# Half-row pairs for one term of two units, a split logarithm and a new step order in a convolution and feed-forward kernel

## Chip, cores and metric

The kernel runs on one core of a Trainium2 chip. The metric is the device time of one execution in microseconds (us). TensorE is called PE here (its weight loads PEld), VectorE DVE, ScalarE ACT, GpSimd POOL, and SyncE, which only issues DMAs in this kernel, SP.

## What is computed

An input of 8 x 4096 tokens with 192 features passes a causal convolution with 7 taps, whose weights are a softmax for each of 8 heads (24 features per head). Then comes a feed-forward layer with a rational function between its two products:

```python
w = np.exp(w - max(w)); w = w / (np.sum(w) + 1e-9)          # per head, over 7 taps
out = np.einsum('hk,bskhg->bshg', w, x_unf)                  # convolution, 192 features per token
x = out.reshape(32768, 192)
h = x @ w_in                                                 # 192 -> 2048
P = a[0] + a[1]*h + a[2]*h**2 + a[3]*h**3
Q = 1.0 + abs(b[0])*abs(h) + abs(b[1])*h**2
g = P / (Q + 1e-6)
y = g @ w_out                                                # 2048 -> 192
```

## The kernel before

The 32768 tokens are cut into 64 **chunks** of 512 tokens, and the 2048 columns of the hidden layer into 8 **units** of 256, as two halves j = 0, 1 of 128. A step is written as kind, number, piece and chunk. In a chunk the following happens.

The convolution (`conv_step`, step `c`, L312) multiplies banded weights with blocks of the input. It splits the array by `tile_position` into two row halves of 64 and four column groups of 32: 72 f32 matmuls of 58 (at the end 48) columns, each of them two instructions, in eight parts. ACT rounds its result to `xh0`, `xh1` (step `xh`, L330), DVE takes the remainder `xl` (step `xl`, L339), and 14 small DMAs (`gaps`, `move`, L352) put the features in order. `X[c, "A"]` holds the rounded features 0 to 127, `X[c, "L"]` their remainders. `X[c, "B"]` holds the rounded features 128 to 191 in rows 0 to 63 and their remainders in rows 64 to 127; the weights of these features stand in both row halves.

The first product (`gemm1`, steps `g1` + unit + piece: `g15b` is unit 5, half 1; L369) has **five terms** of 128x128 weights and 512 columns for each half: high weights with A, low weights with A, high weights with L, high weights with B, low weights with B. They are summed in one PSUM bank of `hp`; `ps_h` has two buffers, so unit k needs the buffer of unit k-2.

Each unit's `hp` goes through `hs` (ACT copy, L410), `p` and `u` (POOL, L413, L417), `A` and `B` (ACT, L424, L427), `v` (DVE, L421, the last reader of `hp`), `Q` (a DMA issued by POOL that adds B to A, L430), `L` (ACT, logarithm over 1024 columns, L433), `Y` (ACT, exponential, L436), `m`, `e`, `g` (DVE, L440, L444, L448). A step `g` + unit without a piece, as `g1.2`, is the DVE step; `g1` with a piece, as `g16a`, is the first product, and `g2` with a piece, as `g20a`, the second one (`gemm2`, L387), with f32 weights and 192 columns, 16 instructions per unit. `O` is the evacuation of the output (ACT, L397; DMA by SP, L398).

The order of all steps on PE, ACT, DVE and POOL is written out by hand, as text: `START` for the first chunks with the preparation of the weights (steps `w..`; L284 is one of them, and their scratch buffers are those of the convolution from chunk 1 on), `PLAN`, repeated for each chunk i from 3 to 62, and `END`. In PLAN the number behind the point says how many chunks the step is late: `c0.0` is the convolution of chunk i, `g15b.1` belongs to chunk i-1, `g16a.2` to chunk i-2. So PE runs `... g15a.1 g15b.1 | c0.0 g16a.2 g16b.2 ...` at the border of two rounds. Each engine executes its steps in the order of the text and waits only for what a step reads or overwrites. In END the number counts back from chunk 64.

Of the kernel before, what the change touches and what calls it, by code (L numbers as in the profile page):

```python
# [41 lines left out]


PLAN = """
c0.0 xh0.0 xh1.0 g16a.2 g16b.2 m2.2 L3.2 xl0.0 xl1.0 B5.2 A5.2 g20b.2 e2.2 g2.2 p5.2 u5.2 g20a.2 hs6.2
Y3.2 g20c.2 g21a.2 g21c.2 v5.2 Q5.2 p6.2 A6.2 u6.2 g20d.2 m3.2 g17a.2 g17b.2 e3.2 g22a.2 L4.2 g3.2 B6.2
hs7.2 v6.2 g21b.2 Y4.2 g21d.2 g22b.2 L5.2 m4.2 Q6.2 e4.2 B7.2 A7.2 g10a.1 g10b.1 g4.2 p7.2 g22d.2 g23b.2
g23d.2 g24b.2 hs0.1 u7.2 p0.1 Y5.2 A0.1 v7.2 L6.2 B0.1 m5.2 e5.2 Q7.2 g11a.1 g11b.1 hs1.1 g22c.2 g5.2
u0.1 g23a.2 g23c.2 g24a.2 Y6.2 p1.1 Q0.1 v0.1 g12a.1 g12b.1 g24d.2 B1.1 A1.1 L7.2 m6.2 e6.2 g6.2 hs2.1
g25b.2 u1.1 Q1.1 p2.1 Y7.2 v1.1 B2.1 m7.2 u2.1 e7.2 g24c.2 g25a.2 A2.1 g13a.1 g13b.1 L0.1 g7.2 hs3.1  # L50
Q2.1 Y0.1 p3.1 g25c.2 g26a.2 v2.1 g26c.2 g27a.2 m0.1 L1.1 A3.1 g14a.1 g14b.1 B3.1 u3.1 Q3.1 e0.1 g27c.2
# [9 lines left out]
wor0.0 wiw4.0 g10b.0 wio3.0 wod1.0 hs0.0 B0.0 wow2.0 woa1.0 p0.0 u0.0 wip1.0 A0.0 Q0.0 wir3.0 wid4.0
wil1.0 wos1.0 woo1.0 wia4.0 g11a.0 g11b.0 hs1.0 p1.0 tp7.0 B1.0 wor1.0 wip2.0 wis4.0 wio4.0 woa2.0
wil2.0 u1.0 A1.0 Q1.0 wos2.0 woo2.0 v0.0 wih3.0 wip3.0 wiw5.0 wia5.0 wod2.0 L0.0 wow3.0 wis5.0 wor2.0
wil3.0 wiw6.0 wid5.0 Y0.0 wio5.0 woa3.0 wow4.0 g12a.0 wir4.0 g12b.0 v1.0 hs2.0 p2.0 wos3.0 m0.0 B2.0
g13a.0 g13b.0 woo3.0 u2.0 wih4.0 wip4.0 wia6.0 wod3.0 L1.0 wor3.0 wiw7.0 A2.0 e0.0 wis6.0 g0.0 hs3.0
# [5 lines left out]
xh0.2 xh1.2 m3.0 xl0.2 e3.0 g3.0 g20a.0 g20c.0 B6.0 hs7.0 p6.0 u6.0 v6.0 g21a.0 g21c.0 g22a.0 L4.0
g10a.1 g10b.1 xl1.2 g20b.0 Q6.0 p7.0 g20d.0 Y4.0 g21b.0 u7.0 m4.0 B7.0 g21d.0 g22b.0 wor4.0 A7.0 Q7.0
L5.0 L6.0 e4.0 hs0.1 g4.0 Y5.0 wod5.0 v7.0 g11a.1 p0.1 m5.0 e5.0 u0.1 wod6.0 B0.1 A0.1 g11b.1 Q0.1 hs1.1
p1.1 A1.1 g5.0 Y6.0 v0.1 m6.0 e6.0 g22c.0 g23a.0 L7.0 u1.1 g22d.0 g23b.0 wor6.0 g6.0 g23d.0 B1.1 g12a.1
v1.1 g12b.1 A2.1 Q1.1 hs2.1 Y7.0 g23c.0 g24a.0 g24b.0 g24d.0 m7.0 e7.0 L0.1 g7.0 g24c.0 g13a.1 g13b.1
# [8 lines left out]
A5.3 u5.3 B5.3 Q5.3 hs6.3 g2.3 v5.3 Y3.3 g17a.3 L4.3 p6.3 g17b.3 u6.3 A6.3 g21a.3 g21c.3 B6.3 Q6.3 hs7.3
p7.3 m3.3 e3.3 g3.3 g22a.3 u7.3 Y4.3 g22c.3 v6.3 g10a.2 B7.3 g10b.2 L5.3 A7.3 Q7.3 hs0.2 p0.2 u0.2 m4.3
e4.3 g4.3 g22b.3 g22d.3 g23a.3 Y5.3 A0.2 v7.3 g11a.2 L6.3 B0.2 g11b.2 g23b.3 g23d.3 g24b.3 hs1.2 p1.2
m5.3 e5.3 g5.3 v0.2 Q0.2 g23c.3 Y6.3 A1.2 g12a.2 m6.3 g12b.2 u1.2 B1.2 Q1.2 g24d.3 e6.3 g6.3 L7.3 v1.2
g24a.3 hs2.2 p2.2 g25b.3 g25d.3 Y7.3 m7.3 g13a.2 g13b.2 g24c.3 g25a.3 g25c.3 g26a.3 e7.3 g7.3 B2.2 A2.2
u2.2 v2.2 g14a.2 L0.2 Q2.2 hs3.2 Y0.2 m0.2 p3.2 L1.2 A3.2 g14b.2 g26b.3 e0.2 g26c.3 g27a.3 g0.2 B3.2
u3.2 v3.2 Q3.2 hs4.2 Y1.2 m1.2 e1.2 g1.2 L2.2 A4.2 g27c.3 O0.3 g15a.2 g15b.2 g20a.2 p4.2 u4.2 B4.2  # L90
g26d.3 g27b.3 hs5.2 Y2.2 g27d.3 v4.2 g16a.2 g16b.2 B5.2 Q4.2 O1.3 m2.2 e2.2 p5.2 u5.2 g2.2 A5.2 Q5.2
v5.2 g20c.2 g21a.2 L3.2 g20b.2 g20d.2 hs6.2 p6.2 u6.2 Y3.2 m3.2 e3.2 g3.2 L4.2 g17a.2 g17b.2 B6.2 A6.2
Q6.2 v6.2 g21b.2 g21d.2 hs7.2 Y4.2 m4.2 g21c.2 L5.2 e4.2 g4.2 p7.2 u7.2 A7.2 B7.2 v7.2 Q7.2 g10a.1
g10b.1 hs0.1 p0.1 u0.1 Y5.2 L6.2 g22a.2 g22c.2 g23a.2 g23c.2 A0.1 g11a.1 m5.2 e5.2 g11b.1 B0.1 hs1.1
g22b.2 p1.1 g5.2 g22d.2 g23b.2 Y6.2 g23d.2 A1.1 v0.1 L7.2 g12a.1 B1.1 g12b.1 hs2.1 m6.2 e6.2 g6.2 Q0.1
Y7.2 B2.1 L0.1 g24b.2 g24d.2 g25b.2 u1.1 v1.1 Q1.1 g13a.1 g13b.1 m7.2 e7.2 p2.1 u2.1 g24a.2 A2.1 g24c.2
g7.2 v2.1 g14a.1 hs3.1 p3.1 g14b.1 Y0.1 m0.1 e0.1 B3.1 Q2.1 L1.1 g25d.2 g26b.2 g0.1 A3.1 g25a.2 u3.1
hs4.1 v3.1 g15a.1 Q3.1 Y1.1 B4.1 g15b.1 m1.1 e1.1 g1.1 L2.1 A4.1 p4.1 u4.1 v4.1 hs5.1 g25c.2 g26a.2 Y2.1
m2.1 e2.1 g2.1 Q4.1 g26c.2 g27a.2 p5.1 u5.1 A5.1 B5.1 v5.1 g27c.2 Q5.1 g26d.2 g16a.1 L3.1 Y3.1 m3.1 e3.1
g27b.2 g16b.1 g17a.1 g27d.2 hs6.1 O0.2 g20a.1 p6.1 g17b.1 A6.1 O1.2 g20b.1 g20d.1 g20c.1 g21a.1 g21b.1  # L100
L4.1 g3.1 Y4.1 m4.1 g21d.1 hs7.1 e4.1 g4.1 B6.1 B7.1 g21c.1 g22a.1 L5.1 Y5.1 g22b.1 u6.1 v6.1 g22c.1
g23a.1 g22d.1 g23b.1 Q6.1 g23d.1 g24b.1 p7.1 u7.1 m5.1 e5.1 g5.1 A7.1 L6.1 v7.1 Y6.1 Q7.1 g24d.1 g25b.1
m6.1 e6.1 g6.1 L7.1 Y7.1 m7.1 e7.1 g23c.1 g24a.1 g24c.1 g7.1 g25a.1 g25c.1 g26a.1 g26c.1 g25d.1 g26b.1
# [266 lines left out]

# [190 lines left out]
```

## Time and profile before

| | us |
|---|---|
| median of 3 runs | 2677.01 |
| the runs | 2675.80 to 2678.11 |
| the profiled execution | 2675.36 |
| its span, first to last instruction | 2673.7 |
| PE busy | 2636.4 |
| DVE busy | 2583.7 |
| ACT busy | 2563.2 |
| POOL busy | 2313.4 |
| mean granted TensorE clock | 0.995 of full speed |

Matmuls are pipelined, and the ends that the profile shows for them are modelled: for PE the distance from one start to the next counts. The figures of DVE and ACT are unions of overlapping instructions.

### The profile page before, as it was taken

The numbers are of one execution on the slowest core, as the hardware profiler recorded it, in microseconds if no ns is written. First come the engines' busy times: TensorE is split into PE (matmuls) and PEld (weight loads), VectorE is DVE, ScalarE is ACT, GpSimd is POOL, SyncE is SP. The second block draws the span as 40 slices with busy tenths as digits, with TensorE's granted clock in tenths as the row PEclk, the third lists the DMA queues.
The fourth block names the chain that finished last, engine by engine and source line by source line (L and its number), as shares of the span: only waits on it lengthen the run. The fifth ranks groups of instructions, "written<-read, shape, count | busy, mean of one in ns | idle before, by whom it ended". The sixth has DMA issues, their size and how long they took to land.

```text
span 2673.7 us, 56816 instructions
## 1 busy us (share of the span) xinstructions
PE 2636.4 (99%) x22513; PEld 2392.6 (89%) x22513; DVE 2583.7 (97%) x2235; ACT 2563.2 (96%) x2863; POOL 2313.4 (87%) x1565
## 2 busy tenths in 40 slices
...
GB/s 198 118 137 127 131 139 125 134 136 125 137 130 130 137 124 131 139 126 132 137 127 137 126 132 136 124 135 135 129 131 134 131 137 123 131 138 124 130 125 93
DMA packets 138706, 352.25 MB, mean 132 GB/s; under 512 B 19416, under 2 KB 54488, under 8 KB 138440
## 3 DMA queue, kind: packets, MB, share of 16 engines
...
q10 hardware_dynamic: 288, 0.03, 0.0%
...
## 4 chain that ended last, share of the span: by engine, by line
PE 92%; DVE 2%; ACT 2%; issue 2%; POOL 1%; DMA 1%; ACTq 0%; POOLq 0%; DVEq 0%
PE o L387 47%; PE hp L369 42%; PE o L312 3%; DVE t L421 1%; DVE y L444 1%; POOL t L417 1%; ACT y L436 0%; ACT hs L410 0%; ACT B L433 0%; DVE t L448 0%; ACT A L424 0%; POOL t L413 0%; ACT B L427 0%; DMA A<-B 0%; PE y L321 0%
## 5 line engine op out<-in xcount | busy, mean ns | idle before, releaser
L387 PE MATMUL o<-wo_t,t 128*128 128x192 f32 x8192 | 1404.2, 326 | 1.3 <-DVE t L448 1.3
L387 PEld LDWEIGHTS o<-wo_t,t 128*128 128x128 f32 x8192 | 1354.2, 190 | 37.2 <-DVE t L448 1.9
L417 POOL TENSOR_TENSOR t<-t,hs 128x1024 f32<-128x1024 f32 x512 | 1264.1, 2469 | 32.2
L369 PE MATMUL hp<-xh,wh_t 128*128 128x512 f32 x2048 | 868.5, 424 | 9.3 <-DVE t L421 5.5
L413 POOL TENSOR_SCALAR t<-hs,cf 128x1024 f32<-128x1024 f32 x512 | 665.0, 1299 | 195.7 <-ACT hs L410 190.9
L369 PE MATMUL hp<-xh,wl_t 128*128 128x512 f32 x2048 | 803.1, 392 | 2.6 <-DVE wl_t L299 1.9
L440 DVE SCALAR_TENSOR_TENSOR t<-t,cf,y 128x1024 f32<-128x1024 f32 x512 | 655.7, 1281 | 34.3 <-ACT y L436 25.4
L421 DVE SCALAR_TENSOR_TENSOR t<-t,cf,hp 128x1024 f32<-128x1024 f32 x512 | 652.4, 1274 | 4.4 <-ACT y L436 2.3
L448 DVE SCALAR_TENSOR_TENSOR t<-y,t 128x1024 f32<-128x1024 f32 x512 | 626.8, 1224 | 17.4
L444 DVE SCALAR_TENSOR_TENSOR y<-A,y 128x1024 f32<-128x1024 f32 x512 | 625.6, 1222 | 0.0
L410 ACT COPY hs<-hp 128x1024 f32<-128x1024 f32 x512 | 519.5, 1015 | 61.9 <-PE hp L369 23.2
L430 POOL DMA_DIRECT2D A<-B x512 | 468.4, 915 | 102.8 <-ACT B L427 69.1
L436 ACT ACTIVATE y<-B 128x1024 f32<-128x1024 f32 x512 | 531.3, 1038 | 20.0 <-DVE t L448 18.5
L433 ACT ACTIVATE B<-A 128x1024 f32<-128x1024 f32 x512 | 545.2, 1065 | 4.0 <-DMA A<-B 3.9
L424 ACT ACTIVATE A<-hp 128x1024 f32<-128x1024 f32 x512 | 528.0, 1031 | 0.8 <-PE hp L369 0.8
L427 ACT ACTIVATE B<-hp 128x1024 f32<-128x1024 f32 x512 | 528.4, 1032 | 0.0
L369 PEld LDWEIGHTS hp<-xh,wh_t 128*128 128x128 f32 x2048 | 387.1, 189 | 84.0 <-DVE t L421 6.7
L369 PEld LDWEIGHTS hp<-xh,wl_t 128*128 128x128 f32 x2048 | 387.1, 189 | 66.0 <-DVE wl_t L299 2.4
L369 PE MATMUL hp<-xl,wh_t 128*128 128x512 f32 x1024 | 401.7, 392 | 0.0
L369 PEld LDWEIGHTS hp<-xl,wh_t 128*128 128x128 f32 x1024 | 193.2, 189 | 42.6 <-issue 0.4
L312 PEld LDWEIGHTS o<-wb_t,xs 64*32 64x32 f32 x9072 | 92.7, 105 | 29.3 <-issue 27.1
L312 PE MATMUL o<-wb_t,xs 64*32 64x58 f32 (+1 forms) x9072 | 102.0, 221 | 6.9 <-issue 3.9
...
## 6 DMA issues: line engine op xcount, KB each, us to landing
A<-B POOLq DMA_DIRECT2D x512, 512.0 KB, 4.8
...
out<-ob SPq DMA_DIRECT2D x128, 192.0 KB
...
```

The costliest lines, as they stand in the source:

```text
L369: nc.tensor.matmul(H[k][:, j, :], lhsT=w[:, i, part, j, :], rhs=x, start=(n == 0), stop=(n == len(terms) - 1))
L387: nc.tensor.matmul(op[:, t, 0:D], lhsT=g[:, j * CH + tok:j * CH + tok + P], rhs=wo_t[:, f, :], start=(f == 0 and t == 0), stop=(f == FT - ...
L413: nc.gpsimd.tensor_scalar(tile_of(k, "t", tpool), st[k]["hs"], a3, a2, ALU.mult, ALU.add)
L417: nc.gpsimd.tensor_tensor(out=t, in0=t, in1=st[k]["hs"], op=ALU.mult)
L421: nc.vector.scalar_tensor_tensor(out=t, in0=t, scalar=a1, in1=flat(k), op0=ALU.add, op1=ALU.mult)
L424: nc.scalar.activation(out=tile_of(k, "A", work), in_=flat(k), func=AF.Abs, scale=scales[0])
L427: nc.scalar.activation(out=tile_of(k, "B", work), in_=flat(k), func=AF.Square, scale=scales[1])
L433: nc.scalar.activation(out=st[k]["B"], in_=st[k]["A"], func=AF.Ln, bias=C_Q)
L436: nc.scalar.activation(out=tile_of(k, "y", ps_y), in_=st[k]["B"], func=AF.Exp, scale=-1.0)
L440: nc.vector.scalar_tensor_tensor(out=t, in0=t, scalar=a0, in1=st[k]["y"], op0=ALU.add, op1=ALU.mult)
L444: nc.vector.scalar_tensor_tensor(out=y, in0=st[k]["A"], scalar=C_Q, in1=y, op0=ALU.add, op1=ALU.mult)
L448: nc.vector.scalar_tensor_tensor(out=t, in0=st[k]["y"], scalar=2.0, in1=t, op0=ALU.subtract, op1=ALU.mult)
```

## The change

For the units 5 and 6 (`HALF_UNITS`) `gemm1` leaves out the fifth term. A new step `h` + unit computes it as a pair of matmuls, one for each half j, of 64 rows each: half 0 with the low weights and B in rows 0 to 63, half 1 with the low weights in rows 64 to 127 and a copy of B's upper rows, `xu`, in rows 64 to 127. The product of the low weights with the remainders, which the full fifth term had in its lower rows, is left out in these units. The copy is one more DMA per chunk, behind the moves of `xl`. The logarithm of unit 3 becomes two ACT instructions of 512 columns (`L3` and `Lz3`). The order of all steps is written anew in START, PLAN and END.

```diff
+HALF_UNITS = (5, 6)
+SPLIT = ("L", 3)
...
 PLAN = """
-c0.0 xh0.0 xh1.0 g16a.2 g16b.2 m2.2 L3.2 xl0.0 xl1.0 B5.2 A5.2 g20b.2 e2.2 g2.2 p5.2 u5.2 g20a.2 hs6.2
...
-g25d.2 g0.1 g26b.2 g26d.2 hs4.1 g27b.2 g27d.2 Y1.1 L2.1 p4.1 O0.2 A4.1 O1.2 u4.1 v3.1 m1.1 e1.1 g1.1
-B4.1 g15a.1 g15b.1 Y2.1 v4.1 hs5.1 Q4.1
+c0.0 g1.2 Lz3.2 Y2.2 hs5.2 v4.2 m2.2 A5.2 h6.2 xh0.0 g16a.2 Q4.2 e2.2 xh1.0 p5.2 xl0.0 L3.2 xl1.0 B5.2
+g16b.2 g20a.2 hs6.2 g2.2 g20c.2 g21a.2 g21c.2 g22a.2 Y3.2 u5.2 p6.2 v5.2 g17a.2 g17b.2 B6.2 g20b.2
...
+g0.1 L1.1 g14a.1 g14b.1 u3.1 A3.1 hs4.1 g27c.2 v3.1 Y1.1 Q3.1 g25b.2 g25d.2 p4.1 g26b.2 m1.1 g26d.2
+g27b.2 g27d.2 A4.1 O0.2 g15a.1 u4.1 g15b.1 e1.1 L2.1 h5.1 B4.1 O1.2
...
 START = """
-c0.1 Y2.0 m2.0 A4.0 hs5.0 p4.0 xh0.1 xh1.1 u4.0 v4.0 g16a.0 Q4.0 p5.0 u5.0 xl0.1 xl1.1 e2.0 B5.0 woa6.0
-A5.0 wos6.0 woo6.0 woa7.0 g2.0 wos7.0 g16b.0 woo7.0 L3.0 c0.2 Q5.0 hs6.0 v5.0 g17a.0 Y3.0 g17b.0 A6.0
...
+wir7.0 wow7.0 wih7.0 woa5.0 wos5.0 woo5.0 wip7.0 B4.0 A4.0 g15b.0 p4.0 u4.0 wil7.0 Q3.0 L2.0 e1.0 h5.0
+hs5.0 p5.0 u5.0 c0.1 xh0.1 v4.0 h6.0 xh1.1 xl0.1 xl1.1 B5.0 g1.0 woa6.0 wos6.0 woo6.0 g16a.0 g16b.0 A5.0
+v5.0 hs6.0 g17a.0 woa7.0 wos7.0 woo7.0 Q4.0 L3.0 Y2.0 B6.0 wod5.0 c0.2 xh0.2 xh1.2 g17b.0 m2.0 e2.0 A6.0
...
 END = """
+Q4.3 g1.3 Lz3.3 Y2.3 hs5.3 v4.3 m2.3 e2.3 L3.3 c0.1 xh0.1 xh1.1 h6.3 g16a.3 A5.3 B5.3 p5.3 u5.3 g16b.3
...
+Q3.2 g14a.2 g14b.2 L1.2 hs4.2 p4.2 Y1.2 m1.2 e1.2 g1.2 A4.2 g26a.3 B4.2 g26c.3 g27a.3 g15a.2 g15b.2 h5.2
...
+h6.2 g16a.2 g16b.2 hs6.2 Y3.2 g20a.2 g20c.2 u5.2 v5.2 Q5.2 B6.2 m3.2 e3.2 g3.2 p6.2 u6.2 g21a.2 g21c.2
...
+e1.1 g1.1 g24b.2 g24d.2 v4.1 g15b.1 h5.1 g25b.2 O0.2 L2.1 Y2.1 m2.1 g20a.1 e2.1 g2.1 g25d.2 h6.1 g16a.1
...
+    zpool = ctx.enter_context(tc.tile_pool(name="zpool", bufs=2))
...
             gaps(xB[BLK:], xl, 104, 2)
+            upper_copy(c)
+
+    def upper_copy(c):
+        X[c, "U"] = zpool.tile([P, CH], F32R, name="xu")
+        move(X[c, "U"][BLK:], X[c, "B"][0:BLK])
...
+    terms_done = {}
+
+    def term(k, j, w, x, **kw):
+        if k not in H:
+            H[k] = ps_h.tile([P, 2, CH], F32, name="hp")
+        n = terms_done[k, j] = terms_done.get((k, j), 0) + 1
+        nc.tensor.matmul(H[k][:, j, :], lhsT=w, rhs=x, start=(n == 1), stop=(n == 5), **kw)
 
     def gemm1(k, j):
         c, i = divmod(k, UPC)
         xhA, xlA, xB = X[c, "A"], X[c, "L"], X[c, "B"]
-        if j == 0:
-            H[k] = ps_h.tile([P, 2, CH], F32, name="hp")
-        terms = ((wh_t, 0, xhA), (wl_t, 0, xhA), (wh_t, 0, xlA), (wh_t, 1, xB), (wl_t, 1, xB))
-        for n, (w, part, x) in enumerate(terms):
-            nc.tensor.matmul(H[k][:, j, :], lhsT=w[:, i, part, j, :], rhs=x, start=(n == 0), stop=(n == len(terms) - 1))
+        for w, part, x in ((wh_t, 0, xhA), (wl_t, 0, xhA), (wh_t, 0, xlA), (wh_t, 1, xB)):
+            term(k, j, w[:, i, part, j, :], x)
+        if i not in HALF_UNITS:
+            term(k, j, wl_t[:, i, 1, j, :], xB)
+
+    def gemm1_halves(k):
+        c, i = divmod(k, UPC)
+        for j, x in enumerate((X[c, "B"], X[c, "U"])):
+            rows = slice(BLK * j, BLK * j + BLK)
+            term(k, j, wl_t[rows, i, 1, j, :], x[rows], tile_position=(BLK * j, 0))
...
-    def step_L(k):
-        nc.scalar.activation(out=st[k]["B"], in_=st[k]["A"], func=AF.Ln, bias=C_Q)
+    def step_L(k, cols=None):
+        cols = cols or (slice(0, CH) if k % UPC == SPLIT[1] else slice(0, W))
+        nc.scalar.activation(out=st[k]["B"][:, cols], in_=st[k]["A"][:, cols], func=AF.Ln, bias=C_Q)
+
+    def step_Lz(k):
+        step_L(k, slice(CH, W))
...
+            elif kind == "h":
+                gemm1_halves(c * UPC + n)
```

## Rows read from the trace of the kernel before

**Rows 1.** Page: engines' busy time, share and instructions; the last-ended chain by engine.

```profile
PE 2636.4 (99%) x22513; PEld 2392.6 (89%) x22513; DVE 2583.7 (97%) x2235; ACT 2563.2 (96%) x2863; POOL 2313.4 (87%) x1565
...
PE 92%; DVE 2%; ACT 2%; issue 2%; POOL 1%; DMA 1%; ACTq 0%; POOLq 0%; DVEq 0%
```

**Rows 2.** One stretch: length; busy PE, PEld, DVE, ACT, POOL (instructions); clock, DMA.

```profile
1000.00:1040.78 40.78, 40.78 (x354) 37.20 (x353) 40.03 (x35) 39.62 (x45) 35.82 (x25) 1.00 0.64 132
```

**Rows 3.** Waits of the steady part, 107 to 2559 us: total us, times, longest.

```profile
PEld o L312 <- issue: 21.1, 58, 0.8
...
ACT hs L410 <- PE hp L369: 17.3, 58, 1.2
...
PE hp L369 <- DVE t L421: 1.8, 3, 0.8
```

**Rows 4.** L312, 100 to 2565 us: count, duration in ns, first and last start.

```profile
L312 PE MATMUL o<-wb_t,xs x8784: 199/211/236, 106.3 to 2560.3; 64*32 64x58 f32 x172, 64*32 64x48 f32 x28
```

**Rows 5.** Time order of PE around a convolution: start us, length us, instruction.

```profile
1004.67 0.39 PE L369 MATMUL hp<-xh,wl_t 128*128 128x512 f32 x1
1004.98 1.59 PE L312 MATMUL o<-wb_t,xs 64*32 64x58 f32 x144
1006.51 0.50 PE L369 MATMUL hp<-xh,wh_t 128*128 128x512 f32 x1
1006.84 0.39 PE L369 MATMUL hp<-xh,wl_t 128*128 128x512 f32 x1
```

**Rows 6.** Time order of PE over one unit.

```profile
1012.68 0.53 PE L369 MATMUL hp<-xh,wh_t 128*128 128x512 f32 x1
1013.05 0.40 PE L369 MATMUL hp<-xh,wl_t 128*128 128x512 f32 x1
...
1014.87 0.39 PE L369 MATMUL hp<-xh,wl_t 128*128 128x512 f32 x1
1015.10 2.76 PE L387 MATMUL o<-wo_t,t 128*128 128x192 f32 x16
1017.56 0.53 PE L369 MATMUL hp<-xh,wh_t 128*128 128x512 f32 x1
```

**Rows 7.** Time order of weight loads (PEld) after a convolution.

```profile
1006.50 0.19 PEld L369 LDWEIGHTS hp<-xh,wh_t 128*128 128x128 f32 x1
1006.61 0.19 PEld L369 LDWEIGHTS hp<-xh,wl_t 128*128 128x128 f32 x1
```

**Rows 8.** Stretch at another convolution's start, PE at L312 alone.

```profile
1045.75:1045.99 0.24, 0.22 (x31) 1.00 0.58 192
```

**Rows 9.** Time order of DVE, then of ACT, around the convolution of rows 5.

```profile
1004.58 1.28 DVE L421 SCALAR_TENSOR_TENSOR t<-t,cf,hp 128x1024 f32<-128x1024 f32 x1
...
1006.60 1.08 ACT L330 CAST xh<-o 128x512 fp32r<-128x512 f32 x2
1007.56 1.07 ACT L433 ACTIVATE B<-A 128x1024 f32<-128x1024 f32 x1
```

**Rows 10.** Time order of SP, which issues DMAs, over one chunk.

```profile
1002.28 1.68 SPq L398 DMA_DIRECT2D out<-ob  x2
...
1016.18 3.67 SPq L352 DMA_DIRECT2D xh<-xl  x4
```

**Rows 11.** START: time order of PE, then the stretch from 60 to 70.

```profile
58.45 0.29 PE L312 MATMUL o<-wb_t,xs 64*32 64x58 f32 x2
61.73 1.82 PE L312 MATMUL o<-wb_t,xs 64*32 64x58 f32 x128 [2.99 <-DVE wo_t L284]
66.00 0.41 PE L312 MATMUL o<-wb_t,xs 64*32 64x48 f32 x14 [2.46 <-issue]
66.34 0.79 PE L369 MATMUL hp<-xh,wh_t 128*128 128x512 f32 x1
...
68.64 0.63 PE L369 MATMUL hp<-xh,wh_t 128*128 128x512 f32 x1
...
60.00:70.00 10.00, 5.81 (x151) 4.81 (x152) 6.75 (x8) 5.55 (x7) 4.46 (x4) 0.60 0.50 100
```

More of the change, by code (lines that the diff above doesn't have):

```diff
@@ L44 @@
 PLAN = """
-c0.0 xh0.0 xh1.0 g16a.2 g16b.2 m2.2 L3.2 xl0.0 xl1.0 B5.2 A5.2 g20b.2 e2.2 g2.2 p5.2 u5.2 g20a.2 hs6.2
[L46 to L49, printed above, removed]
@@ new lines @@
+g20d.2 g21b.2 L4.2 m3.2 Q5.2 A6.2 g21d.2 e3.2 g3.2 hs7.2 Y4.2 A7.2 u6.2 v6.2 m4.2 g10a.1 g10b.1 L5.2
+p7.2 Q6.2 B7.2 e4.2 u7.2 g4.2 v7.2 g22c.2 g23a.2 g23c.2 g22b.2 Q7.2 hs0.1 Y5.2 m5.2 g11a.1 g11b.1 g24a.2
+A0.1 p0.1 g24c.2 B0.1 u0.1 e5.2 L6.2 g5.2 hs1.1 Y6.2 B1.1 A1.1 g22d.2 Q0.1 v0.1 m6.2 g23b.2 p1.1 u1.1
+g12a.1 g12b.1 g23d.2 g24b.2 L7.2 hs2.1 e6.2 Q1.1 g6.2 Y7.2 g25a.2 g25c.2 v1.1 B2.1 A2.1 m7.2 g13a.1
+g13b.1 p2.1 u2.1 L0.1 Q2.1 g26a.2 g26c.2 e7.2 g7.2 v2.1 hs3.1 Y0.1 m0.1 g24d.2 B3.1 p3.1 e0.1 g27a.2
@@ L61 @@
[L61 to L65, printed above, removed]
@@ L71 @@
[L71 to L75, printed above, removed]
@@ L76 @@
-wor5.0 B2.1 p2.1 wod7.0 u2.1 hs3.1 A3.1 wor7.0 g25a.0 g25c.0 g26a.0 g25b.0 g26c.0 Y0.1 v2.1 m0.1 e0.1
-g0.1 g14a.1 g14b.1 g25d.0 B3.1 L1.1 hs4.1 Y1.1 Q2.1 g26b.0 g26d.0 g27a.0 B4.1 g27b.0 g27d.0 g27c.0 p3.1
-u3.1 A4.1 v3.1 g15a.1 L2.1 O0.0 O1.0 m1.1 e1.1 Q3.1 p4.1 g15b.1 u4.1 g1.1 Y2.1 v4.1 Q4.1 hs5.1
+tp8.0 tp1.0 tp3.0 tp9.0 tp2.0 tp5.0 tp4.0 tp6.0 c0.0 cf0.0 cf1.0 wia0.0 wis0.0 wio0.0 cf2.0 xh0.0 wid0.0
+wir0.0 xl0.0 xh1.0 xl1.0 wia1.0 wis1.0 wio1.0 wow0.0 wid1.0 wih0.0 wil0.0 wia2.0 wir1.0 wid2.0 wod0.0
```

68 lines of the change are left out of this document (37 added, 31 removed).

## The prediction

> **What bounds the kernel now.** The page comes first: TensorE (PE) is busy for 99% of the span, and the chain that ended last runs over PE for 92% of it [rows 1]. A busy share can hide slack, so the next view is one chunk from the middle. In 40.78 us PE is never idle, at the full granted clock; VectorE (DVE) has 0.75 us left, ScalarE (ACT) 1.16 us, GpSimd (POOL) 4.96 us [rows 2]. The waits of the steady part agree: in 2452 us PE waits for a release of `hp` by L421 for a few microseconds only, and the one large entry that names no releaser, 58 times at L312, is its own change of layout, priced below [rows 3]. ACT on the other hand waits for PE at L410 once per chunk [rows 3]. The convolution of chunk 3 starts at 106.3 us, and the last instruction of that of chunk 63 at 2560.3 [rows 4]; with the 1.4 us of the last one taken off (from 1004.98 to 1006.51 in [rows 5], less the change of layout at its end), 60 chunks take 2452.6 us, 40.88 each. So a nanosecond taken off PE in each chunk is a nanosecond of the period, while at most 0.75 us goes.
>
> **The pairs: what goes.** A full matmul of 512 columns follows the one before it after 0.2275 us: eight steps from 1013.05 to 1014.87 [rows 6]. In units 5 and 6 the fifth term was two of these; four go in each chunk, 4 x 0.2275 = 0.91 us.
>
> **What a pair costs.** No row shows a 64x128 half, so I build it from the nearest ones. *Do two row halves overlap?* L312 splits the array by rows too. An f32 instruction of 192 columns holds PE 0.163 us (a unit's stretch of 4.88 us, from 1012.68 to 1017.56, less ten full matmuls leaves 2.605 us for sixteen [rows 6]), so one of 58 columns holds its part of the array 0.049 us. In the first 0.22 us that PE is busy with a convolution 31 of them start [rows 8]. Four column groups alone would need 31/4 x 0.049 = 0.38 us; eight parts, with both row halves working, need 0.19. They overlap, and I take a pair at the time of one matmul, 0.2275. The other bound is no overlap, 0.455.
>
> *Its weight load.* After the convolution the first full matmul lasts until 1006.84, 0.33 us instead of 0.23 [rows 5]: the load of its weights begins with it, and the next load follows 0.11 us later [rows 7]. Inside a run this load is hidden; after a change of layout it is bare. A pair opens a layout, so it pays 0.11 (bounds: 0 if the load is drawn ahead, 0.22 if the second half's load waits for the first's). The Trainium skill's "TensorE: Matmul & The Clock Gate", section "LDWEIGHTS (loading the stationary operand)", says that a load's time goes with its columns and not its rows; by that half a load of 128 columns costs as much as a whole one, and the sum stays.
>
> *The change of layout.* The last full matmul starts at 1004.67 and the convolution at 1004.98: 0.31, where the next full one would have come after 0.23. So the change costs 0.09 with nothing to wait for [rows 5]. The new order stands as `g15b.1 h5.1 | c0.0 h6.2 g16a.2`: the two pairs lie on both sides of the convolution. The old two changes (full to split, split to full) stay, once each, and two new ones appear, 64x128 to 64x32 and back. Their price, s, lies between 0 (both layouts cut the rows in the same halves) and 0.09 (every change drains); below 0 it can't lie, since a layout more lets nothing start earlier. I take 0.09, the only price that a row shows. The Trainium skill's "TensorEngine Tiling (Array Packing)", section "Key Properties", speaks against this change: it says that a change of tiling mode, and not just of tile, drains the TensorE. No run here shows a change between two split layouts; by that rule s is 0.09, without it 0.
>
> *Sum for one chunk.* Added 2 x (0.11 + 0.2275 + 0.09) = 0.855, removed 0.91: gain **0.055 us**. With s = 0 it is 0.235; with the loads hidden as well 0.455. There are 61 such places (units 5 and 6 of chunks 1 to 61; chunk 0's lie in START, where PE isn't the bound): **-3.4 us**, with -14.3 and -27.8 for the cheaper layouts.
>
> **END.** Units 5 and 6 of the last two chunks get no convolution beside them. A pair in the midst of full matmuls pays 0.09 + 0.11 + 0.2275 + 0.09 + 0.11 = 0.63 for the 0.455 removed: 4 x 0.17 = **+0.7 us**.
>
> **The split logarithm.** L433 of 1024 columns lasts 1.07 us, two ACT instructions of 512 columns together 1.08 [rows 9]. By that Lz and L cost some 0.01 to 0.1 us more per chunk; ACT's 1.16 us of idle time covers it. Without the cover it would be at most 61 x 0.1 = 6 us. Its first half stands ahead of `Y2 hs5`, where ACT waits for PE anyway [rows 3].
>
> **The copy `xu`.** One more DMA on SP's queue, 128 KB per chunk, behind the 14 moves that SP issues until 1019.85 [rows 10]. At the pace of the last four (3.67/4) it takes 0.92 us more; the next `out<-ob` in SP's queue comes a period after that at 1002.28 [rows 10]. It waits for `h6` two chunks back, which runs before `xl1`, and its reader `h5` comes a whole chunk later. Cost nothing; a late copy would block SP's queue, not PE.
>
> **The order.** v4 (DVE) must free the `hp` buffer for the first matmul of unit 6, now `h6`. DVE still runs m1, e1, g1, v4, m2 in this place. v4 ends at 1005.86 [rows 9], the matmul comes at 1006.51; with `h5` (0.11 + 0.23 + 0.09, less 0.455 that left unit 5) the convolution shifts by -0.03, so the 0.65 us of slack stay. The chunk's other DVE, ACT and POOL steps move by a place or two, within their idle time; I set this at 0, with +3 us as the bound (a wait of 0.05 per chunk).
>
> **START.** The convolution of chunk 2 meets a hole: it starts at 58.45, goes on at 61.73 when L284 has freed its second buffer, stops once more until 66.00, and only then come g17a and g17b, slowly, at 66.34 and 68.64 [rows 11]; the granted clock from 60 to 70 is 0.60 of full speed [rows 11]. In the new START g17a stands ahead of `c0.2`, and the L284 before it isn't later (v5 now stands ahead of it on DVE, but g1 has taken the place of e2 and g2). Five matmuls move into the hole: 1.14 us at full clock, 2.3 as they ran; I take **-1.7 us**, bounds -4 and +3 (the whole START is ordered anew).
>
> **Sum.** -3.4 + 0.7 - 1.7 = -4.4 us. The profiled execution took 2675.36 us, 1.7 around its span of 2673.7, so 2671.0; it lies 1.65 below the median of the runs (2677.01), so the forecast is **2672.6 us**. Its own range, from START and the order, is 2668 to 2678. About 0.2% (5.4 us) is what a measurement can tell from no change.
>
> **Rivals.**
> *Split layouts change freely.* With s = 0 the gain is 61 x 0.235 = 14.3, with the loads hidden too 27.8; with the -1.0 of START and END that is **2662** and 2648. For it: both layouts halve the rows, so no part of the array changes its rows. Against: both changes that the trace shows cost 0.09 or a bare load.
> *The second half runs late.* Place: the two halves of a pair. If the second one's load waits for the first's, a pair costs 0.11 more: 122 x 0.11 = +13.4, **2686**; with no overlap of the streams 122 x 0.2275 = +27.8, 2700. It decides as soon as a pair is late by more than 0.03 us (0.455 - 0.4275). For it: over the whole convolution, 144 instructions in 1.4 us, the overlap isn't complete (144/8 x 0.049 = 0.88). Against: its first 31 do overlap.
> *Another engine takes the place.* DVE's 0.75 us caps the gain at 61 x 0.75 = 46 us, beyond all these cases, but waits along the new order could eat the little that is forecast: **2677**. Against: the steps around the edge stand as before.
>
> **How the numbers follow.** Forecast 0.48 (0.20 of it under 2671.6, the rest within 0.2%), free changes 0.30 (all faster), late halves 0.17 (0.15 slower, 0.02 within), another engine 0.05 (within, 0.01 slower). Faster 0.50, same 0.34, slower 0.16. The range 2655 to 2686 takes in the forecast, the first rival down to half-hidden loads and the second one with a late load; full hiding and no overlap stay outside.
>
> **What would show it.** In the changed trace, from the last full matmul of `g15b` to `h5`, 0.31; from `h5` to the first L312, 0.43 (0.34 if changes are free, 0.54 if the load is late); the second half's start beside the first's; the convolutions 40.83 us apart on average (40.65 if free, 41.05 if late), PE still never idle; ACT's waits at L410 unchanged. PE waits inside a chunk for L421 or L448 beyond a few microseconds in all would show that the order, not the pairs, set the time, and my sum wrong.

## The result and the profile after

The changed kernel takes **2692.08 us** in the median (2689.26 to 2694.32, six runs) against 2677.53 for the kernel before on the same chip: a ratio of 1.0054, interval 1.0041 to 1.0067. It is 14.5 us slower, above the whole range of the forecast. The profiled execution took 2692.22 us, with a span of 2690.5, 16.8 more than before. In the new line numbers L316 is the convolution, L377 the first product with the pairs, L409 the second product, L432 `hs`, L443 `v`, L452 `Q`, L344 `xl`.

First the page, as in [rows 1] (busy time, share and instructions; a queue's packets, MB and share of the DMA engines):

```profile
PE 2641.1 (98%) x22513; PEld 2367.5 (88%) x22513; DVE 2582.0 (96%) x2235; ACT 2561.3 (95%) x2927; POOL 2299.2 (85%) x1565
...
q8 instruction: 177, 2.90, 0.4%
```

The convolutions of the steady part, as in [rows 4]:

```profile
L316 PE MATMUL o<-wb_t,xs x8784: 202/211/236, 105.6 to 2576.6; 64*32 64x58 f32 x172, 64*32 64x48 f32 x28
```

Chunk 3 begins 0.7 us earlier than in [rows 4], and the last instruction of the last convolution 16.3 us later: in these two executions START gained 0.7, END lost some 0.5, and the steady part lost 17.0, of which more below. Next the waits of the steady part (total us, times, longest), to be set beside [rows 3]:

```profile
ACT hs L432 <- PE hp L377: 46.6, 62, 2.5
...
PEld hp L377 <- issue: 41.5, 122, 3.1
...
PEld o L409 <- issue: 8.3, 7, 2.0
PE o L409 <- issue: 6.2, 7, 1.7
PE hp L377 <- issue: 4.5, 3, 2.6
...
PEld hp L377 <- DVE t L443: 1.7, 3, 1.0
```

PE hardly waits for another engine. ACT waits more for PE than in [rows 3], so the other engines are further from the bound than before. But PE stands still, up to 3 us at a time, with "issue" as the only name: it waited for nothing that the profile shows. The one of this name in [rows 3] was at most 0.8 us long. (Most of the 122 at L377 are the pairs' own changes of layout, 0.36 us ahead of `h5` and 0.24 behind `h6`.)

One of these stalls, in the time order of PE (start us, length us, instruction, idle time before it):

```profile
1008.98 0.39 PE L377 MATMUL hp<-xh,wh_t 128*128 128x512 f32 x1
1009.30 0.49 PE L377 MATMUL hp<-xh,wl_t 64*128 64x512 f32 x1
1009.30 0.49 PE L377 MATMUL hp<-xu,wl_t 64*128 64x512 f32 x1
1009.73 1.60 PE L316 MATMUL o<-wb_t,xs 64*32 64x58 f32 x144
1011.25 0.50 PE L377 MATMUL hp<-xh,wl_t 64*128 64x512 f32 x1
1011.26 0.50 PE L377 MATMUL hp<-xu,wl_t 64*128 64x512 f32 x1
1011.69 0.50 PE L377 MATMUL hp<-xh,wh_t 128*128 128x512 f32 x1
...
1013.64 2.11 PE L409 MATMUL o<-wo_t,t 128*128 128x192 f32 x12
1016.18 1.08 PE L409 MATMUL o<-wo_t,t 128*128 128x192 f32 x5 [0.44 <-issue]
```

The pairs cost what the forecast said: 0.32 us from the last full matmul to `h5`, 0.43 from there to the convolution, and 0.44 from `h6` to the next full matmul. What was not forecast stands in the last line: a run of the second product breaks off in its midst, 6.5 us behind the convolution.

**What PE waits for.** The queue q8 of the page carries instructions, that is, the program itself: 177 packets in the span, each 16,384 bytes by the trace's DMA records. The trace has 45,425 PE instructions (weight loads, matmuls, 399 of the sequencer), and 177 x 256 = 45,312, so I take a packet to be 256 PE instructions; that the gaps come at one place modulo 256, as follows, bears it out. I numbered PE's instructions in order of time and looked at each gap of more than 0.5 us between two matmuls in the steady part. Of 16 such gaps 13 stand at the same place of a packet: the last instruction before the gap is number 449 + 256 n, where n is the number of the packet that had started last (counted from 0). In twelve of them PE goes on 1.2 to 1.6 us behind the end of that packet. In the trace of before 5 of 8 gaps stand there, none of the five above 0.9 us. So PE has used up what it was sent and waits for the next packet.

The 13th gap, in chunk 29, only looks alike. PE goes on 2.5 us behind the end of its packet there, and the trace names another releaser, DVE's remainder of the convolution:

```profile
1178.51 0.76 PE L409 MATMUL o<-wo_t,t 128*128 128x192 f32 x3 [0.66 <-DVE xl L344]
```

The same wait stands in chunk 29 of e1, e3, e4 and e12 below, wherever the packets lie.

The packet is late because of the transfers around it; e3 and e5 below bear on this. Two stretches of the DMA view in the chunk above (queue, kind: packets, MB, share of the 16 engines), first from 1010.3 to 1012.8 and then from 1013.0 to 1014.0:

```profile
q0 software_dynamic: 121, 0.50, 113.0%
...
q1 hardware_dynamic: 97, 0.34, 88.4%
q8 instruction: 1, 0.02, 6.0%
q0 software_dynamic: 16, 0.00, 5.2%
```

q0 is `Q4`'s A<-B (L452, issued 1008.49): in this window of 2.5 us no other queue moves anything. From 1009.73 to 1011.25 PE runs the 288 instructions of the convolution, in 1.5 us. The packet starts at 1013.77, 4.0 us behind the convolution's start and 0.9 behind the end of the transfer, when PE is already 428 instructions beyond its border (number 256 n). In the kernel before, `Q4` was issued 0.21 us ahead of the convolution and its transfer lay 1.2 to 4.1 us behind the convolution's start; and the packets that started with PE more than 350 instructions beyond their border did so 1.4 us behind the convolution's start in the median. In the new order `Q4` is issued 1.24 us ahead, its transfer lies at 0.5 to 3.1, and such packets start at 4.0 us in the median. A chunk is 710 PE instructions, 58 less than three packets, so a packet's border comes back to nearly the same place of the chunk after 4 or 5 chunks: the stalls stand 4 or 5 chunks apart, but for chunks 29 and 42, where the trace shows none.

**Where the 17.0 us are.** A chunk without stalls takes 40.82 us instead of 40.78: 60 x 0.041 = 2.5. The gaps at the place 449 + 256 n (all of more than 0.1 us over the usual pitch) are 15.9 us instead of 3.8: 12.1. Other gaps are 4.9 instead of 2.5: 2.4. With chunk 29's wait of 0.8 us put among the others it is 11.3 and 3.2.

### The profile page after: what moved, and what is told of

It is laid out like the page before. It is cut to its first block, busy times and chain, and to the rows that moved or that the text cites. A ratio compares the mean times of both kernels' runs of the same rounds, so it can differ in the third digit from the quotient of the medians.

```text
span 2690.5 us, 56950 instructions
## 1 busy us (share of the span) xinstructions
PE 2641.1 (98%) x22513; PEld 2367.5 (88%) x22513; DVE 2582.0 (96%) x2235; ACT 2561.3 (95%) x2927; POOL 2299.2 (85%) x1565
## 4 chain that ended last, share of the span: by engine, by line
PE 91%; issue 2%; ACT 2%; DVE 2%; POOL 2%; DMA 1%; ACTq 0%; POOLq 0%; DVEq 0%; SPq 0%
PE o L409 46%; PE hp L377 41%; PE o L316 3%; POOL t L439 1%; DMA A<-B 1%; ACT y L462 1%; DVE y L470 0%; POOL t L435 0%; DVE t L443 0%; ACT hs L432 0%; ACT A L446 0%; DVE t L474 0%; DVE t L466 0%; ACT B L449 0%; ACT B L456 0%
## 5 line engine op out<-in xcount | busy, mean ns | idle before, releaser
L409 PE MATMUL o<-wo_t,t 128*128 128x192 f32 x8192 | 1408.0, 326 | 7.5 <-issue 6.2
L409 PEld LDWEIGHTS o<-wo_t,t 128*128 128x128 f32 x8192 | 1355.5, 190 | 46.8 <-issue 8.8
L435 POOL TENSOR_SCALAR t<-hs,cf 128x1024 f32<-128x1024 f32 x512 | 647.9, 1265 | 255.3 <-ACT hs L432 250.6
L377 PE MATMUL hp<-xh,wh_t 128*128 128x512 f32 x2048 | 849.5, 425 | 14.8 <-DVE t L443 10.2
L377 PE MATMUL hp<-xh,wl_t 128*128 128x512 f32 (+1 forms) x1920 | 767.0, 399 | 2.8 <-DVE wl_t L303 1.1
L443 DVE SCALAR_TENSOR_TENSOR t<-t,cf,hp 128x1024 f32<-128x1024 f32 x512 | 652.4, 1274 | 3.9 <-POOL t L439 2.7
L432 ACT COPY hs<-hp 128x1024 f32<-128x1024 f32 x512 | 521.5, 1019 | 92.2 <-PE hp L377 52.2
L456 ACT ACTIVATE B<-A 128x1024 f32<-128x1024 f32 (+1 forms) x576 | 566.1, 983 | 9.3 <-DMA A<-B 9.2
L452 POOL DMA_DIRECT2D A<-B x512 | 463.2, 905 | 73.3 <-ACT B L449 40.6
L377 PEld LDWEIGHTS hp<-xh,wh_t 128*128 128x128 f32 x2048 | 386.5, 189 | 103.1 <-issue 25.4
L377 PEld LDWEIGHTS hp<-xh,wl_t 128*128 128x128 f32 (+1 forms) x1920 | 362.0, 189 | 85.4 <-issue 24.8
L377 PE MATMUL hp<-xl,wh_t 128*128 128x512 f32 x1024 | 403.3, 394 | 2.6 <-issue 2.6
L377 PEld LDWEIGHTS hp<-xl,wh_t 128*128 128x128 f32 x1024 | 192.9, 188 | 45.7 <-issue 3.1
L316 PEld LDWEIGHTS o<-wb_t,xs 64*32 64x32 f32 x9072 | 92.5, 105 | 19.8 <-issue 19.3
L316 PE MATMUL o<-wb_t,xs 64*32 64x58 f32 (+1 forms) x9072 | 101.5, 220 | 3.9 <-issue 3.9
```

Source lines behind the costliest of these rows:

```text
L377: nc.tensor.matmul(H[k][:, j, :], lhsT=w, rhs=x, start=(n == 1), stop=(n == 5), **kw)
L409: nc.tensor.matmul(op[:, t, 0:D], lhsT=g[:, j * CH + tok:j * CH + tok + P], rhs=wo_t[:, f, :], start=(f == 0 and t == 0), stop=(f == FT - ...
L435: nc.gpsimd.tensor_scalar(tile_of(k, "t", tpool), st[k]["hs"], a3, a2, ALU.mult, ALU.add)
L443: nc.vector.scalar_tensor_tensor(out=t, in0=t, scalar=a1, in1=flat(k), op0=ALU.add, op1=ALU.mult)
L456: nc.scalar.activation(out=st[k]["B"][:, cols], in_=st[k]["A"][:, cols], func=AF.Ln, bias=C_Q)
```

## The experiments

The table has, for each kernel's profiled execution, the median distance of two convolutions in the steady part, the gaps at the packets' borders (number 449 + 256 n, with one instruction to either side) and the other gaps, all worked out from the starts of PE's instructions as above. The packet gaps of after, e1, e3 and e4 hold chunk 29's wait of 0.8 us. Each ratio is to runs of the kernel before on the same chip.

| kernel | median us | ratio to before | chunk us | packet gaps us | other gaps us |
|---|---|---|---|---|---|
| before | 2677.53 | | 40.78 | 3.8 | 2.5 |
| after | 2692.08 | 1.0054 | 40.82 | 15.9 | 4.9 |
| e1_no_pairs | 2694.67 | 1.0062 [1.0045, 1.0079] | 40.85 | 15.0 | 6.5 |
| e2_pairs_old_order | 2675.41 | 0.9991 [0.9982, 1.0001] | 40.73 | 7.4 | 2.2 |
| e11_pairs_again | 2675.67 | 0.9993 [0.9984, 1.0002] | 40.75 | 8.2 | 2.4 |
| e3_small_q4 | 2681.57 | 1.0016 [1.0006, 1.0025] | 40.80 | 6.3 | 5.1 |
| e4_late_q4 | 2694.51 | 1.0067 [1.0050, 1.0084] | 40.96 | 5.6 | 15.2 |
| e5_early_q4_old_order | 2682.89 | 1.0023 [1.0013, 1.0032] | 40.80 | 11.7 | 3.4 |
| e6_later_b4 | 2702.24 | 1.0090 [1.0073, 1.0107] | 41.12 | 3.7 | 28.3 |
| e7_later_b4_runs24 | 2732.98 | 1.0203 [1.0186, 1.0220] | 41.66 | 10.0 | 51.9 |
| e8_split_log_old_order | 2677.67 | 0.9999 [0.9989, 1.0008] | 40.78 | 7.1 | 3.2 |
| e9_run20_old_order | 2686.67 (one run) | | 40.93 | 5.6 | 8.2 |
| e10_pairs_late_q4 | 2680.44 | 1.0010 [1.0001, 1.0019] | 40.75 | 6.6 | 6.6 |
| e12_shift_29 | 2700.60 (one run) | | 40.80 | 19.0 | 6.5 |

The packet gaps are not the same in two executions of the same order: before, e8 and the pairs in the old order show 3.8 to 8.2. A difference of less than some 4 us in this column says little.

### The pairs or the order?

e1: the new order without the pairs.

```diff
-HALF_UNITS = (5, 6)
+HALF_UNITS = ()
...
-            upper_copy(c)
...
-g27b.2 g27d.2 A4.1 O0.2 g15a.1 u4.1 g15b.1 e1.1 L2.1 h5.1 B4.1 O1.2
+g27b.2 g27d.2 A4.1 O0.2 g15a.1 u4.1 g15b.1 e1.1 L2.1 B4.1 O1.2
```

> The changed kernel in its new order, with five full terms in all units: no pairs, no copy xu. Theory I (instruction fetch): in the changed trace the pairs cost what was forecast, 0.43 us each, and the loss is stalls of PE that no engine's release ends, about 20 us in all against 7 before; each ends 2.2 to 2.7 us after a packet of the instruction queue q8 started, and those packets start late, because the transfer of Q4 (512 KB), which the new order puts 0.5 to 3.1 us behind the start of a convolution, fills the DMA engines just when PE has used up some 290 instructions in 1.5 us. So the stalls stay without the pairs: 2686 to 2692 us, PE's idle time without a releaser 15 us or more. Theory II (the pairs themselves, or the copy xu, make the stalls): 2675 to 2680, idle time as before.

e2: the pairs alone, in the old order.

```diff
-c0.0 xh0.0 xh1.0 g16a.2 g16b.2 m2.2 L3.2 xl0.0 xl1.0 B5.2 A5.2 g20b.2 e2.2 g2.2 p5.2 u5.2 g20a.2 hs6.2
+c0.0 xh0.0 xh1.0 h6.2 g16a.2 g16b.2 m2.2 L3.2 xl0.0 xl1.0 B5.2 A5.2 g20b.2 e2.2 g2.2 p5.2 u5.2 g20a.2 hs6.2
...
-B4.1 g15a.1 g15b.1 Y2.1 v4.1 hs5.1 Q4.1
+B4.1 g15a.1 g15b.1 h5.1 Y2.1 v4.1 hs5.1 Q4.1
```

> The kernel before in its old order, with the pairs alone: h5 behind g15b, h6 ahead of g16a, the copy xu; the logarithm whole. Theory I: Q4 stays where it was, so the stalls stay at about 7 us, and the pairs change the period by -0.05 to +0.03: 2674 to 2680 us. Theory II (pairs or copy): 2688 to 2693.

e11 is e2 once more.

> The same kernel as e2_pairs_old_order, in more rounds, to tell 0.1% from nothing: the undisturbed chunk was 40.733 us there against 40.780, 61 x 0.047 = 2.9 us, less some 0.7 for END; with the stalls equal 2674 to 2676 us, ratio 0.999.

The waits of PE at the second product, first of e1, then of e2:

```profile
PEld o L407 <- issue: 8.5, 7, 2.2
PE o L407 <- issue: 6.3, 6, 1.9
```

```profile
PEld o L408 <- issue: 0.7, 1, 0.7
```

The whole loss is there without the pairs (e1 lies 2.7 us above the range expected), and with the pairs alone it is gone. So it comes from the order. The pairs shorten a chunk by 0.047 us (0.033 in e11) where 0.055 was forecast, which is 2.0 to 2.8 us in 60 chunks; the two kernels measure 2.4 and 1.9 us less than before, with intervals that just take in no change.

### The split logarithm

e8: the kernel before with `Lz3` ahead of `L3`.

```diff
-c0.0 xh0.0 xh1.0 g16a.2 g16b.2 m2.2 L3.2 xl0.0 xl1.0 B5.2 A5.2 g20b.2 e2.2 g2.2 p5.2 u5.2 g20a.2 hs6.2
+c0.0 xh0.0 xh1.0 g16a.2 g16b.2 m2.2 Lz3.2 L3.2 xl0.0 xl1.0 B5.2 A5.2 g20b.2 e2.2 g2.2 p5.2 u5.2 g20a.2 hs6.2
```

> The kernel before in its old order with the logarithm of unit 3 alone in two halves, one behind the other. The forecast's price is nothing, since ACT has 1.16 us of idle time per chunk: 2675 to 2680 us. If ACT is closer to the bound than its idle share says: up to 6 us more, 2683.

It costs nothing: 0.9999, and the chunk stays at 40.78 us.

### Q4's transfer

e3: the changed kernel with `Q4` cut to 64 of its 1024 columns from chunk 3 on.

```diff
-        nc.gpsimd.dma_start(out=st[k]["A"], in_=st[k]["B"], accum_op=ALU.add)
+        cols = slice(0, 64 if k % UPC == 4 and k >= 3 * UPC else W)
+        nc.gpsimd.dma_start(out=st[k]["A"][:, cols], in_=st[k]["B"][:, cols], accum_op=ALU.add)
```

> The changed kernel, in which Q4 adds only 64 of 1024 columns from chunk 3 on (the rest of unit 4's denominator lacks its square term). Theory I: without that transfer the instruction packets start in time and the stalls go nearly all: 2670 to 2677 us, PE's idle time without a releaser under 6 us. Theory II: no change, 2688 to 2693. A third one, that the new order lets PE wait for other engines, also says no change.

e4: `Q4` whole, but behind `p5`; e5: the other way round, `Q4` issued some 0.4 us earlier in the old order, by way of `O1`.

```diff
-c0.0 g1.2 Lz3.2 Y2.2 hs5.2 v4.2 m2.2 A5.2 h6.2 xh0.0 g16a.2 Q4.2 e2.2 xh1.0 p5.2 xl0.0 L3.2 xl1.0 B5.2
+c0.0 g1.2 Lz3.2 Y2.2 hs5.2 v4.2 m2.2 A5.2 h6.2 xh0.0 g16a.2 e2.2 xh1.0 p5.2 Q4.2 xl0.0 L3.2 xl1.0 B5.2
```

```diff
-g25d.2 g0.1 g26b.2 g26d.2 hs4.1 g27b.2 g27d.2 Y1.1 L2.1 p4.1 O0.2 A4.1 O1.2 u4.1 v3.1 m1.1 e1.1 g1.1
-B4.1 g15a.1 g15b.1 Y2.1 v4.1 hs5.1 Q4.1
+g25d.2 g0.1 g26b.2 g26d.2 hs4.1 g27b.2 g27d.2 Y1.1 L2.1 p4.1 O0.2 A4.1 u4.1 v3.1 m1.1 e1.1 g1.1
+B4.1 O1.2 g15a.1 g15b.1 Y2.1 v4.1 hs5.1 Q4.1
```

> The changed kernel with one step moved in PLAN: Q4 behind p5 instead of ahead of it on POOL, so that its transfer starts some 3.5 us behind the start of the convolution and not 0.5. Theory I: the instruction packets slip in ahead of it, the stalls fall to the level of before or below: 2673 to 2681 us. Theory II and the third one: 2688 to 2694. If L4 comes late by it, waits of ACT for the transfer appear, and up to 0.1 us per chunk.

> The kernel before, without pairs, with one step moved in PLAN: O1 behind B4 on ACT, so that B4 and with it Q4 come some 0.4 us sooner, toward where the new order has them (1.24 us ahead of the convolution's start; the old order 0.2). Theory I (instruction packets stuck behind Q4's transfer): PE's idle time without a releaser grows from about 7 us to 10 to 20, 2680 to 2691 us. If the place of Q4 is not the cause but something else of the new order: 2676 to 2679, stalls as before.

The waits of e3, then of e4:

```profile
PEld o L409 <- issue: 0.5, 1, 0.5
```

```profile
ACT B L456 <- DMA A<-B: 49.2, 61, 2.2
...
DVE t L443 <- POOL t L439: 42.5, 62, 0.7
...
PEld hp L377 <- DVE t L443: 13.8, 33, 1.1
```

Without `Q4`'s bytes the packet gaps fall by 9.6 us, from 15.9 to 6.3, and the time by some 10, to 1.0016; packets with PE more than 350 instructions ahead start 1.4 us behind the convolution again. The time stays 4.6 us above the range expected, since the other gaps and the longer chunk of the new order remain. With `Q4` later the packet gaps fall to 5.6, but the time doesn't, and lies 13.5 us above its range: the logarithm of unit 4 now waits for the sum, POOL's `u` comes later, and PE waits for `v`.

In e5 such packets start at 2.1 us, the packet gaps grow to 11.7 us, and the kernel is 6 us slower, as expected, but hardly by `Q4`: by the trace's DMA records its transfer begins 1.17 us behind the convolution's start, where the kernel before has 1.25. What moved is the output's transfer, which goes with `O1`: it lies at 0.4 to 1.1 us instead of -0.5 to 0.2. In the old order the DMA engines stand nearly free between the two transfers, from 0.2 to 1.25 us; in e5 and in the new order (output's transfer up to 0.5, `Q4`'s from 0.5) the two follow one another closely. So e3 shows that `Q4`'s bytes delay the packets, and e5 points to the output's transfer as a second cause, which no run tests by itself.

Two attempts to take the transfer out of the way by a later `B4` went wrong: e6, and e7, which also regroups the second product.

```diff
-c0.0 g1.2 Lz3.2 Y2.2 hs5.2 v4.2 m2.2 A5.2 h6.2 xh0.0 g16a.2 Q4.2 e2.2 xh1.0 p5.2 xl0.0 L3.2 xl1.0 B5.2
+c0.0 g1.2 Lz3.2 B4.2 Y2.2 hs5.2 v4.2 m2.2 A5.2 h6.2 xh0.0 g16a.2 Q4.2 e2.2 xh1.0 p5.2 xl0.0 L3.2 xl1.0 B5.2
...
-g27b.2 g27d.2 A4.1 O0.2 g15a.1 u4.1 g15b.1 e1.1 L2.1 h5.1 B4.1 O1.2
+g27b.2 g27d.2 A4.1 O0.2 g15a.1 u4.1 g15b.1 e1.1 L2.1 h5.1 O1.2
```

> The changed kernel with one step moved: B4 behind Lz3 on ACT instead of ahead of O1, so that Q4 is issued some 0.8 us later, about where the old order has it, and still early enough for L4. Theory I: the stalls fall from 20 us to about 7, no new wait of ACT for the transfer: 2677 to 2683 us. If not the place of Q4: 2688 to 2693.

> The kernel of e6_later_b4 with seven steps of the second product moved one place ahead in PLAN, so that its runs of instructions between two first products are 24, 16, 16, 16, 16, 16, 24 as in the old order, and not 20, 16, ..., 28. In the changed trace the full matmuls behind the runs of 20 and 28 follow one another by 0.231 to 0.236 us more often than behind the others, in all 0.07 us per chunk that the old order with the pairs doesn't have. If the length of the runs makes that: 0.05 to 0.07 us per chunk less than e6_later_b4, 3 to 4 us. If something else of the order does: the same time as e6_later_b4.

Both put a convolution's remainder (L344) on PE's path, in e6 as

```profile
PEld o L409 <- DVE xl L344: 31.1, 56, 0.8
```

so their times, far above what was expected, tell nothing of the packets. The packet gaps of e6 are as few as before's (3.7 us).

e10: `Q4` behind `p5` in the old order, with the pairs.

> The old order with the pairs (as in e2_pairs_old_order) and Q4 behind p5 on POOL, so that its transfer starts some 4.4 us behind the start of the convolution and not 1.3. Theory I: the instruction packets meet no large transfer in the first 4 us, PE's idle time without a releaser falls from 8 us to 3 to 5, and if L4 (8.1 us behind the start of the convolution) still finds its data: 2670 to 2674 us. If L4 or u5 comes late, as with e4_late_q4: 2676 to 2690, with waits of ACT for the transfer or of PE for L421.

The packet gaps (6.6 us) stay where e2 and e11 have them, and PE gets new waits, `v` (L442) above all:

```profile
ACT B L455 <- DMA A<-B: 11.9, 19, 1.0
...
PEld hp L376 <- DVE t L442: 6.3, 15, 1.1
```

So a later `Q4` lowers the packet gaps only in the new order, and in neither order did it make the kernel faster.

### The packets by themselves

e12 shifts the borders of the packets and, but for a longer START, nothing else: 29 matmuls (58 PE instructions) ahead of the first one of chunk 0.

```diff
         n = terms_done[k, j] = terms_done.get((k, j), 0) + 1
+        if (k, j, n) == (0, 0, 1):
+            for _ in range(29):
+                nc.tensor.matmul(H[k][:, j, 0:64], lhsT=w, rhs=x[:, 0:64], start=True, stop=True)
```

> The changed kernel with 29 extra matmuls of 64 columns at the very start of chunk 0 (ahead of the first matmul of g10a, which overwrites what they write), and nothing else. With their weight loads they are 58 PE instructions more ahead of the steady part. One chunk is 710 PE instructions, and 710 = 3 x 256 - 58, so 58 more instructions ahead move the place of the 256-instruction packet borders by exactly one chunk. Theory A (PE stalls where a packet of 256 instructions arrives late because its transfer stands behind Q4's A<-B, close behind a convolution): the stalls of the changed kernel at 275.5, 437.3, 646.2, 808.3, 1016.2, 1178.5, 1340.9 and 1549.1 us all move one chunk later, to about 316, 478, 687, 849, 1057, 1220, 1382 and 1590 us (plus what START becomes longer, 0 to 6 us), with nothing left at the old places; total 2690 to 2698 us, some 20 us of stalls as before. Rival B (the stalls come from the transfers alone, A<-B, xs and the moves, which run the same way in each chunk, or from some event in time): they stay in the chunks where they were, at 275.5, 437.3 and so on, plus what START becomes longer; total 2690 to 2698 us as well. Rival C (they fall anywhere, by chance of the DMA engines): no common shift.

The gaps of more than 0.5 us at number 449 + 256 n, by the chunk whose convolution stands before them (from chunk 4 on):

| | chunks |
|---|---|
| after | 7, 11, 16, 20, 25, 29, 33, 38, 47, 51, 55, 60 |
| e12 | 8, 12, 17, 21, 26, 30, 34, 39, 43, 48, 52, 56, 61 |

All but one come one chunk later: eleven of twelve. The exception is chunk 29, whose wait for `xl` is named above. In e12 chunk 29 has this wait again, at another place of a packet (behind number 20,219), and the gap in chunk 30 is one of the packets, as the releasers say. So theory A's sign "nothing left at the old places" fails for this one, which was no packet stall to begin with:

```profile
1183.21 2.06 PE L412 MATMUL o<-wo_t,t 128*128 128x192 f32 x11 [0.68 <-DVE xl L344]
...
1226.46 1.73 PE L412 MATMUL o<-wo_t,t 128*128 128x192 f32 x9 [2.22 <-issue]
```

With chunk 43, e12 has two packet gaps that the changed kernel hasn't. (In chunk 3, right behind START, both have one, after the same number 1729.) The stall of chunk 25, shown above, as e12 has it: chunk 25 runs through, and the run breaks off in chunk 26 at the same instruction of the chunk.

```profile
1018.71 3.42 PE L412 MATMUL o<-wo_t,t 128*128 128x192 f32 x20
...
1059.51 2.12 PE L412 MATMUL o<-wo_t,t 128*128 128x192 f32 x12
1061.84 1.41 PE L412 MATMUL o<-wo_t,t 128*128 128x192 f32 x7 [0.22 <-issue]
```

Nothing in the chunk's transfers was touched; only the count of instructions ahead was. For the eleven that moved, this settles that PE waits for its instructions. The kernel took 2700.6 us, 2.6 above the range expected: chunk 3 begins 4.7 us later, and the gaps are 4.7 us more. The other gaps (in chunks 29, 42 and 55, 0.6 to 1.1 us) stay in their chunks, so they have another cause (one of 0.5 us in chunk 50 has its like, 0.7, in chunk 51 of e12, a wait for `xl`); the kernel before has gaps in these three chunks too, in which PE waits for `v`. What delays the other engines there is open.

### The 0.09 us that are left in each chunk

Against the pairs in the old order, a chunk without stalls is 0.09 us longer in the new order (40.82 to 40.73), and e1 shows it without pairs (0.07). About 0.065 of it stands in full matmuls 0.231 to 0.240 apart instead of 0.2275: some 0.045 right behind longer runs of the second product (the new order has runs of 20 and 28, the old one of 16 and 24), and 0.02 behind `h6`. e9 makes two runs of 20 in the old order:

```diff
-Y3.2 g20c.2 g21a.2 g21c.2 v5.2 Q5.2 p6.2 A6.2 u6.2 g20d.2 m3.2 g17a.2 g17b.2 e3.2 g22a.2 L4.2 g3.2 B6.2
+Y3.2 g20c.2 g21a.2 g21c.2 v5.2 Q5.2 p6.2 A6.2 u6.2 m3.2 g17a.2 g17b.2 g20d.2 e3.2 g22a.2 L4.2 g3.2 B6.2
```

> The kernel before in its old order, no pairs, with one step of the second product (g20d) moved in PLAN from ahead of unit 7's first product to behind it: the run behind the convolution shrinks from 24 instructions to 20, the next one grows from 16 to 20. In the new order the full matmuls behind the runs of 20 and 28 are the slow ones; e7_later_b4_runs24 could not tell, since PE waited for DVE there. If the length of the runs makes them slow: the undisturbed chunk grows from 40.78 us by 0.03 to 0.07, and the full matmuls of units 7 and 0 stand 0.231 to 0.236 apart in more places. If not: 40.78 as before.

The chunk grows by 0.15 us, but not by what was meant. 0.10 of it is a wait of PE for `v` behind one of the runs:

```profile
1015.91 0.19 PEld L369 LDWEIGHTS hp<-xh,wh_t 128*128 128x128 f32 x1 [0.26 <-DVE t L421]
```

The full matmuls behind one run of 20 do stand mostly 0.231 to 0.236 apart, which makes 0.03 us; behind the other run, the one with the wait, they don't. In e11 some behind a run of 24 stand 0.231 to 0.235 apart as well. So the length of the run is not shown to make the slower pitch; its cause is open.

## Why the prediction was wrong

**What failed** is the step "The order. ... I set this at 0, with +3 us as the bound". It counted DVE, ACT and POOL steps against idle time and SP's queue against its own next use. It priced no transfer against another, and put the cost of that at nothing without a reason. `Q4`'s issue moved 1.0 us ahead against the convolution and its transfer 0.7, and the bytes it moves came to lie ahead of PE's own instructions. The queue q8 stands on the page of before as well, and I read past it: 0.4% of the DMA engines' time. By the trace of before, the order cost some 11 us in packets, 3 in other gaps and 60 x 0.09 = 5.4 in the slower pitch and what is left open beside it. That trace had few packet gaps for its order: beside e2 and e11, which have the pairs too, the packets' share is 7 to 8 us.

**"PE is never idle"** [rows 2] was true of the chunk that I looked at, not of all: before lost 3.8 us at packets' borders in others. The mean of 40.88 us from [rows 4] beside the 40.78 of one chunk showed 0.1 us per chunk that I left unexplained.

**The pairs** were right in mechanism and size. A change between the two split layouts costs as much as one from full to split: 0.43 us from pair to convolution is 0.11 + 0.2275 + 0.09, where free changes wanted 0.34. (The sum fits; its three terms were not measured one by one. A load of 64 rows lasts 0.18 us in the trace, one of 128 rows 0.19.) The rival "split layouts change freely" falls with that, and the sentence of the Trainium skill's "TensorEngine Tiling (Array Packing)", section "Key Properties", on draining agrees with this 0.43. The rival "the second half runs late" falls too: in the chunk shown the halves start within 0.01 us. Gain 0.055 forecast, 0.047 and 0.033 measured (e2, e11).

**END** (+0.7 forecast, some +0.5 measured) and the **copy** and the **split logarithm** (nothing) were right. **START**'s gain of 1.7 is not shown: chunk 3 begins at 105.6 us instead of 106.3, but in the traces of the other kernels with the old order at 104.6 to 106.7. The five matmuls of `g17a` did move ahead of the convolution of chunk 2, but waited 2.4 us for `v` there. **The third rival**, waits along the new order, had the right place and the wrong kind: it spoke of engines, capped itself at 2677, and had a chance of 0.05. Its sign to look for was too narrow: PE's waits for L443 are the few microseconds of [rows 3], and the order set the time all the same. The two signs that did speak were "PE still never idle" and "ACT's waits at L410 unchanged": ACT's went from 17.3 us to 46.6 (L432).
